# Holding input loads behind the crossbar transposes of the batch in work

## The chip, the cores and the metric

The kernel runs on one core of a Trainium2 chip. The metric is the device time in microseconds (us) of one execution. Times are medians of several executions, and comparisons use executions in the undisturbed ("fast") state, taken in the same rounds on the same chip. Batches are counted from 0, as in the code: the "batch four" that the prediction mentions is batch 3.

## The reference

Eight batches of attention (8 heads, 576 tokens, head size 64) with a relative bias, followed by a feed-forward layer that takes the largest of three products:

```python
scores = scale * np.matmul(q, k.transpose(0, 1, 3, 2)) + bias      # per batch and head
attn = np.exp(scores - scores.max(-1)); attn /= attn.sum(-1) + 1e-09
attn_out = np.matmul(attn, v)                                       # (8, 8, 576, 64)
x = attn_out.transpose(0, 2, 1, 3).reshape(8 * 576, 512)
h = np.maximum(np.maximum(x @ w1, x @ w2), x @ w3)                  # 512 -> 768
out = h @ w_out                                                     # 768 -> 512
```

## The kernel before

For each batch three kinds of transfer matter here. GpSimd issues the loads of q, k and v from HBM, with a cast from float32 to bfloat16. SyncE issues the crossbar transposes of the loaded q and k into `qT` and `kT`: DMA transfers that turn a tile on its way, four whole tiles and a tail (the last 64 tokens) for each. TensorE computes scores from `qT` and `kT` and products with v. Every load goes through `in_turn`, so GpSimd issues in program order.

```python
def load_qk(b, behind=None):          # 8 tile loads, then the tails of q and k: 11 loads
    ...
    go_behind(loads, behind)          # every load waits for the transfer `behind`

def load_v(b, h0, h1, behind=None):   # 4 tile loads and 2 tails: 6 loads
    ...

def transposes(b):                    # SyncE: tile t of q and of k, five steps
    for t in range(KT + 1):
        one(0, t)                     # records turned_qk[b, 0, t]
        one(1, t)                     # records turned_qk[b, 1, t]
        yield
```

In the main loop over batches b and head pairs hp, the transposes of batch b + 1 are issued step by step during batch b from hp 1 on, the fourth tile (`t = KT - 1`) in the second half of hp 2 and the tail in hp 3. The loads stand between them:

```python
if hp == (2, 1, 0)[min(b, 3) - 1] and b + 1 < B:
    load_v(b + 1, 0, H, turned_qk[2, 1, KT - 1] if b == 1 else None)
if (b, hp) == (2, 0):
    batch[3] = load_tiles()
    load_qk(3, divided[1, HP - 1, 1])
if hp == 2 and 1 < b < B - 2:
    batch[b + 2] = load_tiles()
    load_qk(b + 2)
```

So q and k of batch 4 and later wait for nothing but free buffers and their turn.

The softmax here doesn't subtract the row's maximum and nothing guards it: scores larger than these inputs give would overflow.

Of the kernel before, what the change touches and what calls it, by code (L numbers as in the profile page):

```python
# [39 lines left out]
def kernel(  # L40
# [13 lines left out]
    B, H, S, D = q.shape  # L54
# [8 lines left out]
    KT = 4  # L63
# [63 lines left out]
    def main_part(src, b):  # L127
        return src[b, :, 0 : KT * P, :].rearrange("h (t p) d -> p t h d", p=P)

    def tail_part(src, b, h0, h1, par):  # L130
        return src[b, h0 + par : h1 : 2, KT * P : S, :].rearrange("h p d -> p h d")

    def in_turn(b, load):
        return inorder(load)

    def load_main(src, b, h0, h1, dst, t0=0, t1=KT):
        x = main_part(src, b)
        return [
            in_turn(b, nc.gpsimd.dma_start(out=dst[:, t, h0:h1, :], in_=x[:, t, h0:h1, :])) for t in range(t0, t1)  # L139
        ]  # L140
# [5 lines left out]
    def load_q_tail(b):  # L146
        dst = qtail[b % 2][0 : S - KT * P].rearrange("p g (h d) -> p (g h) d", h=2)
        return in_turn(b, nc.gpsimd.dma_start(out=dst, in_=q[b, :, KT * P : S, :].rearrange("h p d -> p h d")))

    def k_diag(b, par, h0, h1):  # L150
        return diag(ktail[b % 2], par, h0, h1)
# [4 lines left out]
    def load_tail(src, b, h0, h1, dst):  # L156
        return [
            in_turn(b, nc.gpsimd.dma_start(out=dst(b, par, h0, h1), in_=tail_part(src, b, h0, h1, par)))
            for par in range(2)
        ]  # L160

    def load_qk(b, behind=None):

        loads = []
        for t in range(KT):
            for src, dst in zip((q, k), batch[b]):
                loads.append(in_turn(b, nc.gpsimd.dma_start(out=dst[:, t], in_=main_part(src, b)[:, t])))  # L167
        loads.append(load_q_tail(b))
        for par in range(2):
            load = nc.gpsimd.dma_start(out=k_diag(b, par, 0, H), in_=tail_part(k, b, 0, H, par))  # L170
            loads.append(in_turn(b, load))
        go_behind(loads, behind)

    def go_behind(loads, behind):

        for load in loads if behind else ():
            tc.add_manual_dep(
                load.ins, behind.ins.name,
                mybir.DependencyInfo(mybir.DependencyClass.Sync, mybir.DependencyReason.DATA),
                reason="these loads go behind the transposes in line",  # L180
            )

    def load_v(b, h0, h1, behind=None):
        loads = load_main(v, b, h0, h1, vx[b % 2][:, :, :, 0:D])
        go_behind(loads + load_tail(v, b, h0, h1, v_diag), behind)
# [224 lines left out]
    def store_outputs():  # L410

        while stores:
            stores.pop(0)()
# [7 lines left out]
    def early():  # L421

        if pending and None in pending[0][1]:
            n, fns = pending[0]
            i = fns.index(None)
            for fn in fns[:i]:
                fn()
            pending[0] = (n, fns[i + 1 :])
# [16 lines left out]
    def transposes(b):  # L445

        made = qk_tiles()
        qk.append(made)

        def one(j, t):  # L450
            n = P if t < KT or j else S - KT * P
            src = batch[b][j][:, t].rearrange("p h d -> p (h d)") if t < KT else (
                (qtail, ktail)[j][b % 2][0:n].rearrange("p h c -> p (h c)")
            )
            turned_qk[b, j, t] = inorder(nc.sync.dma_start_transpose(out=made[j][:, :, P * t : P * t + n], in_=src))  # L455

        for t in range(KT + 1):
            one(0, t)
            one(1, t)
            yield  # L460
# [59 lines left out]
    def times_band(hp, e4, t, lo, hi, put=lambda x: x):  # L520
        lo, hi = max(lo, P * t - P), min(hi, P * t + 2 * P)
        if lo < hi:
            c0, c1 = BAND - (hi - P * t + P), BAND - (lo - P * t + P)
            put(nc.vector.tensor_tensor(  # L524
                out=e4[:, t, :, lo:hi], in0=e4[:, t, :, lo:hi],
                in1=hank[:, 2 * hp : 2 * hp + 2, c0:c1][:, :, ::-1], op=ALU.mult,
            ))
# [17 lines left out]
    def visit(qT, kT, e4, c, mid=None, el=None):  # L545

        if el is not None:
            banks = [ps_a.tile([P, KT * 64], F32, tag="a", name="scq") for _ in range(2)]
            turn_left_queries(qT, kT, banks)
            put_left_queries(el, banks)  # L550
        for tt in range(0, KT, 2):
            sc = ps_s.tile([P, 2, 2, QS], F32, tag="sc", name="sc")
            for t in range(2):
                for par in range(2):
                    r = slice(64 * par, 64 * par + 64)
                    mm(
                        sc[:, par, t, :], lhsT=kT[r, P * (tt + t) : P * (tt + t) + P],
                        rhs=qT[r, c * QS : c * QS + QS],
                    )
            exp(e4[:, tt : tt + 2, :, c * QS : c * QS + QS].rearrange("p t h q -> p h t q"), sc[:])  # L560
            if tt == 0 and mid:
                mid()
# [30 lines left out]
    divided, turned_qk = {}, {}  # L593
# [62 lines left out]
    def x_tile():  # L656
        return xs.tile([P, KT + 1, d_model], BF16, tag="x_sb", name="x_sb")
# [3 lines left out]
    def next_late():  # L661
        return late.pop(0)() if late else (lambda: None)

    def e_tiles():
        return (
            ep.tile([P, KT, 2, QM], BF16, tag="e4", name="e4"),
            ep.tile([P, S + KT * P], BF16, tag="el", name="el"),
        )
# [75 lines left out]
    for hp in range(HP):  # L744
# [14 lines left out]
        def keys():  # L759
            left_keys(hp, qT, kT, el, QS, S)  # L760
# [33 lines left out]
    for b, hp in [(b, hp) for b in range(1, B) for hp in range(HP)]:  # L794
        if hp == 0:
            x_sb[b] = x_tile()
        qT, kT = (x[:, hp, :] for x in qk[b])
        e4, el = e_tiles()
        together = b > 1 and (b, hp) != (2, 0)
        rate = 8 if b == 1 or (b, hp) == (2, 0) else 13  # L800



        visit(qT, kT, e4, 0)
        store_outputs()
        if b == 1:
            if hp == 0:
                crossbar = transposes(2)
            next(crossbar, None)
        elif hp and b + 1 < B:  # L810
            if hp == 1:
                crossbar = transposes(b + 1)
            next(crossbar)
        early()
        if turned:
            turned.pop(0)()
        quotients = next_late()
        times_band(hp, e4, 0, 0, QS, inorder)
        quotients()
        if b == 1 and hp + 1 < HP:  # L820
            spread_packed(hp + 1, nc.vector)

        def keys():
            left_keys(hp, qT, kT, el, 0, S)
            if together:
                next_late()()

        fill(rate, keys, *([lambda: None] if together else []))
        times_bandt(hp, el)


        visit(qT, kT, e4, 1, el=el if together else None)
        store_outputs()
        if b == 1 or hp in (1, 2) and b + 1 < B:
            next(crossbar, None)
        early()
        if turned:
            turned.pop(0)()
        if not together:
            quotients = next_late()  # L840
            times_band(hp, e4, 1, 0, QM, inorder)
            quotients()
        if b == 1 and hp + 1 < HP:
            second_transposes(qk[1], hp + 1)
        if hp == 1:
            add_ffn((b - 1) * CH if b > 1 else QS, CH if b > 1 else QS)
        if hp == (2, 1, 0)[min(b, 3) - 1] and b + 1 < B:
            load_v(b + 1, 0, H, turned_qk[2, 1, KT - 1] if b == 1 else None)
        if (b, hp) == (2, 0):
            batch[3] = load_tiles()  # L850
            load_qk(3, divided[1, HP - 1, 1])
        if hp == 2 and 1 < b < B - 2:
            batch[b + 2] = load_tiles()
            load_qk(b + 2)

        def queries():
            if not together:
                left_queries(hp, qT, kT, el)
            times_band(hp, e4, 3, 0, QM, inorder)

        def bands_2():
            for t in range(1 if together else 2, 3):
                times_band(hp, e4, t, 0, QM, inorder)

        fill(rate, bands_2, queries)
        times_band_left(hp, el)
        for half in range(2):
            late.append(lambda b=b, hp=hp, e4=e4, el=el, half=half: attend(b, hp, e4, el, half))
# [44 lines left out]
```

## Time and profile before

| | before |
|---|---|
| median time | 325.49 us (325.08 to 326.58, 3 runs) |
| span of the profiled execution | 324.7 us |
| TensorE busy | 305.5 us (94%) |
| share of 16 DMA engines' span taken by GpSimd's queue | 78.1% |
| landing of a k transpose, median | 8.2 us |
| TensorE's named waits for `kT` | 1.87 + 0.22 us at batch 3, 1.09 us at batch 4 |

How to read it: TensorE carries the time, so an idle stretch of it is worth its length, and idle time of the others is worth nothing. The share of the DMA queue sums the time that the packets took, and it can pass 100%, so it shows crowding and not how much the engines could still move.

### The profile page before, as it was taken

The numbers are of one execution on the slowest core, as the hardware profiler recorded it, in microseconds if no ns is written. First come the engines' busy times: TensorE is split into PE (matmuls) and PEld (weight loads), VectorE is DVE, ScalarE is ACT, GpSimd is POOL, SyncE is SP. The second block draws the span as 40 slices with busy tenths as digits, with TensorE's granted clock in tenths as the row PEclk, the third lists the DMA queues.
The fourth block names the chain that finished last, engine by engine and source line by source line (L and its number), as shares of the span: only waits on it lengthen the run. The fifth ranks groups of instructions, "written<-read, shape, count | busy, mean of one in ns | idle before, by whom it ended". The sixth has DMA issues, their size and how long they took to land.

```text
span 324.7 us, 8194 instructions
## 1 busy us (share of the span) xinstructions
PE 305.5 (94%) x3288; PEld 171.1 (53%) x3328; DVE 214.1 (66%) x535; ACT 201.1 (62%) x297; POOL 108.1 (33%) x143
## 2 busy tenths in 40 slices
PE   7768999999979999899999999999999999999995
PEld 2346777765535555455555555555555554444442
DVE  6476788776665676676777766776667675454452
ACT  4958898886766667576777677767776661121221
POOL 8941980459557561285019500500000000000000
PEclk9979999999999999999999999999999999999999
DMA  9999999999999999999969998997031103301103
GB/s 164 200 206 198 149 134 176 113 119 158 194 164 156 126 197 168 109 117 176 195 73 135 150 192 88 123 202 99 12 75 71 62 2 73 131 0 65 67 0 129
DMA packets 163878, 40.34 MB, mean 124 GB/s; under 512 B 153720, under 2 KB 159360, under 8 KB 163840
## 3 DMA queue, kind: packets, MB, share of 16 engines
q0 software_dynamic: 103776, 16.66, 78.1%
q1 hardware_dynamic: 58304, 22.69, 39.3%
q10 hardware_dynamic: 1760, 0.47, 0.7%
q8 instruction: 26, 0.43, 0.6%
q14 instruction: 12, 0.10, 0.1%
HBM read 35.39 MB, written 9.45 MB: 138 GB/s over the span
## 4 chain that ended last, share of the span: by engine, by line
PE 74%; DMA 8%; SPq 5%; ACT 4%; POOL 3%; DVE 3%; issue 2%; ACTq 0%; POOLq 0%
PE ps L94 38%; PE a L94 12%; PE pso L94 12%; PE sc L94 7%; DMA kT<-ktail 5%; SPq L455 4%; ACT e L530 3%; PE sct L94 2%; DMA vt<-in_v_dram 2%; PE scq L94 2%; DVE e L524 1%; POOL q_sb L139 1%; POOL vx L139 1%; DMA out_dram<-osb 1%; PE tp L97 1%
## 5 line engine op out<-in xcount | busy, mean ns | idle before, releaser
L94 PE MATMUL ps<-xT,w_bf 128*128 128x512 bf16 (+1 forms) x694 | 151.2, 357 | 1.4
L530 ACT ACTIVATE e<-sc 128x1024 bf16<-128x1024 f32 x128 | 124.5, 1033 | 20.5 <-PE sc L94 20.5
L94 PEld LDWEIGHTS <-w_bf 128*128 128x128 bf16 x720 | 65.2, 97 | 64.1 <-issue 8.4
L524 DVE TENSOR_TENSOR e<-e,hank 128x512 bf16<-128x512 bf16 (+2 forms) x136 | 59.0, 470 | 14.3 <-ACT e L530 12.9
L339 ACT ACTIVATE m<-ps 128x512 bf16<-128x512 f32 x54 | 32.9, 609 | 52.3 <-PE ps L94 52.3
L345 DVE TENSOR_TENSOR m<-ps,m 128x512 bf16<-128x512 f32 x54 | 37.1, 687 | 34.0 <-PE ps L94 34.0
L94 PEld LDWEIGHTS <-kT 64*128 64x128 bf16 (+1 forms) x832 | 29.7, 95 | 40.0 <-issue 23.2
L94 PE MATMUL pso<-wo_bf,hT 128*128 128x512 bf16 (+2 forms) x208 | 47.7, 373 | 0.8 <-issue 0.2
L350 DVE TENSOR_TENSOR hT<-ps,m 128x512 bf16<-128x512 f32 x54 | 37.2, 688 | 16.5 <-PE ps L94 15.1
L139 POOL DMA_DIRECT2D vx<-in_v_dram x32 | 28.3, 902 | 59.1 <-PE a L94 44.5
L94 PE MATMUL a<-vx,e 128*128 128x65 bf16 x1024 | 46.0, 195 | 0.0
L94 PE MATMUL sc<-qT,kT 64*128 64x256 bf16 x512 | 40.8, 272 | 4.9 <-DMA kT<-k_sb 1.9
L94 PEld LDWEIGHTS <-e 128*128 128x128 bf16 x1024 | 41.7, 99 | 0.9
L94 PE MATMUL a<-vt,el 128*128 128x130 bf16 x160 | 35.9, 224 | 2.4 <-DMA vt<-in_v_dram 2.4
L110 DVE COPY osb<-pso 128x512 f32<-128x512 f32 (+1 forms) x33 | 22.6, 686 | 18.0 <-PE pso L94 14.3
L530 ACT ACTIVATE el<-scq 128x256 bf16<-128x256 f32 (+1 forms) x55 | 20.5, 416 | 21.3 <-PE scq L94 21.3
L632 DVE TENSOR_TENSOR x_sb<-a,rd 128x256 bf16<-128x256 f32 (+1 forms) x64 | 31.4, 491 | 2.2
L94 PEld LDWEIGHTS <-hT 128*128 128x128 bf16 x222 | 20.1, 98 | 22.4 <-issue 1.5
L94 PEld LDWEIGHTS <-el 128*128 128x128 bf16 x416 | 24.2, 97 | 11.6 <-issue 5.3
L530 ACT ACTIVATE el<-sct 128x576 bf16<-128x576 f32 (+2 forms) x36 | 21.6, 603 | 10.3 <-PE sct L94 9.1
L167 POOL DMA_DIRECT2D q_sb<-in_q_dram x24 | 21.9, 913 | 10.5 <-DMA vx<-in_v_dram 4.0
L167 POOL DMA_DIRECT2D k_sb<-in_k_dram x24 | 21.9, 912 | 9.1 <-DMA vx<-in_v_dram 8.8
(68 smaller groups left out, 156.8 us busy)
## 6 DMA issues: line engine op xcount, KB each, us to landing
out_dram<-osb SPq DMA_DIRECT2D x35, 256.0 KB, 3.0
vx<-in_v_dram POOLq DMA_DIRECT2D x32, 128.0 KB, 6.5
q_sb<-in_q_dram POOLq DMA_DIRECT2D x26, 128.0 KB, 8.4
k_sb<-in_k_dram POOLq DMA_DIRECT2D x24, 128.0 KB, 9.1
w_bf<-in_moe_w_dram POOLq DMA_DIRECT2D x3, 768.0 KB, 13.5
xT<-in_k_dram SPq DMA_DIRECT2D x6, 128.0 KB, 4.9
hank<-w_dr SPq DMA_DIRECT2D x2, 384.0 KB, 6.1
wo_bf<-in_moe_w_out_dram POOLq DMA_DIRECT2D x1, 768.0 KB, 11.9
```

What stands on the lines that cost most here:

```text
L94: inorder(nc.tensor.matmul(*args, **kw))
L97: inorder(nc.tensor.transpose(*args))
L110: return inorder(nc.vector.tensor_copy(out_, in_))
L139: in_turn(b, nc.gpsimd.dma_start(out=dst[:, t, h0:h1, :], in_=x[:, t, h0:h1, :])) for t in range(t0, t1)
L167: loads.append(in_turn(b, nc.gpsimd.dma_start(out=dst[:, t], in_=main_part(src, b)[:, t])))
L339: nc.scalar.activation(out=st[fb]["m0"][:], in_=ps0, func=ACTF.Copy)
L345: inorder(nc.vector.tensor_tensor(out=m[:], in0=ps1, in1=st[fb]["m0"][:], op=ALU.max))
L350: inorder(nc.vector.tensor_tensor(out=hT[:, fb * CH : fb * CH + CH], in0=ps2, in1=st[fb]["m"][:], op=ALU.max))
L455: turned_qk[b, j, t] = inorder(nc.sync.dma_start_transpose(out=made[j][:, :, P * t : P * t + n], in_=src))
L524: put(nc.vector.tensor_tensor(out=e4[:, t, :, lo:hi], in0=e4[:, t, :, lo:hi], in1=hank[:, 2 * hp : 2 * hp + 2, c0:c1][:, :, ::-1], op=ALU. ...
L530: nc.scalar.activation(out=out_, in_=in_, func=ACTF.Exp, scale=inv_sqrt_d)
L632: divided[b, hp, half] = inorder(nc.vector.tensor_tensor(out=x_sb[b][:, 2 * half : 2 * half + n, P * hp : P * hp + P].rearrange("p t (h d) ...
```

## The change

The intent is to keep loads that nobody needs yet from running beside the transposes that TensorE needs next. v of batch 3 moves from hp 1 to hp 2 of batch 2 and waits for the fourth k transpose of batch 3. The q and k of batches 4 to 7 wait for the fourth k transpose of the batch before them.

```diff
-        if hp == (2, 1, 0)[min(b, 3) - 1] and b + 1 < B:
-            load_v(b + 1, 0, H, turned_qk[2, 1, KT - 1] if b == 1 else None)
+        if hp == (2, 2, 0)[min(b, 3) - 1] and b + 1 < B:
+            load_v(b + 1, 0, H, turned_qk[b + 1, 1, KT - 1] if b < 3 else None)
         ...
         if hp == 2 and 1 < b < B - 2:
             batch[b + 2] = load_tiles()
-            load_qk(b + 2)
+            load_qk(b + 2, turned_qk[b + 1, 1, KT - 1])
```

## The prediction

> **What bounds the kernel now.** Batches are numbered from 0 as in the code, so "batch four" of the title is batch 3. I read the page's first two parts, then busy time by stage, then TensorE's own waits, then the chain that ended last around those waits, and last the DMA queues. TensorE is busy 305.5 us of a span of 324.7 at a granted clock of 0.995, so only its idle time can be won. Busy time by stage (columns: window, its length, then busy time of TensorE, weight load, VectorE, ScalarE, GpSimd, clock, DMA share, GB/s):
>
> ```profile
> 75.00:92.00 17.00, 16.32 (x200) 9.11 (x202) 11.48 (x28) 11.91 (x18) 11.30 (x15) 1.00 1.91 180
> 92.00:109.00 17.00, 14.80 (x170) 7.92 (x168) 10.89 (x26) 11.68 (x17) 11.90 (x16) 1.00 2.13 152
> ...
> 126.00:143.00 17.00, 15.81 (x163) 8.01 (x165) 10.90 (x26) 11.68 (x17) 7.87 (x10) 1.00 1.62 128
> 143.00:160.00 17.00, 16.84 (x200) 9.32 (x200) 12.16 (x31) 11.42 (x17) 6.45 (x9) 1.00 1.92 169
> 160.00:177.00 17.00, 16.84 (x198) 9.23 (x198) 11.82 (x29) 12.51 (x19) 7.69 (x10) 1.00 1.21 109
> ```
>
> A settled window has 16.84 of 17, that is 0.16 idle. Two windows have more: 92 to 109 has 2.20 and 126 to 143 has 1.19. From 143 to 262 every such window is settled, so loads there hide nothing that can be won. The first 40 us (8.9 us idle) come before anything the change touches. TensorE's instructions in order show what the two bad windows wait for:
>
> ```profile
> 94.94 0.50 PE L94 MATMUL sc<-qT,kT 64*128 64x256 bf16 x6
> 97.31 0.28 PE L94 MATMUL sc<-qT,kT 64*128 64x256 bf16 x2 [1.87 <-DMA kT<-k_sb]
> ...
> 99.38 0.42 PE L94 MATMUL sct<-qT,kT 128*128 128x512 bf16 x2 [0.22 <-DMA kT<-ktail]
> ```
> ```profile
> 134.22 0.42 PE L94 MATMUL sct<-qT,kT 128*128 128x512 bf16 x2 [1.09 <-DMA kT<-ktail]
> ```
>
> These are the first scores of batch 3 and of batch 4: the fourth tile and the tail of k have not come through the crossbar. Together 1.87 + 0.22 + 1.09 = 3.18 us. The chain at the first of them (start, length, what) shows why:
>
> ```profile
> 86.41 1.21 SPq L455
> 87.72 2.12 SPq L455
> 89.93 1.21 SPq L455
> 91.24 8.10 DMA kT<-ktail
> ```
>
> SyncE issues the transposes back to back here (each starts 0.1 us after the one before ended), and the last takes 8.1 us to land. One issue takes 2.12 and another, at 83.24, 2.45, against the usual 1.2. What that latency is when no loads run, the DMA answers for two stretches say: 107 to 128, beside the q and k loads of batch 5, and 212 to 226, when all loads are over.
>
> ```profile
> kT<-k_sb SPq DMA_TRANSPOSE x4, 8.5
> ```
> ```profile
> kT<-k_sb SPq DMA_TRANSPOSE x3, 2.4
> ```
>
> So the latency is mostly queueing beside the loads. GpSimd's instructions say which loads stand in the way (start, time, load):
>
> ```profile
> 78.49 1.89 POOL L139 DMA_DIRECT2D vx<-in_v_dram  x2
> ...
> 86.29 0.89 POOL L167 DMA_DIRECT2D q_sb<-in_q_dram  x1 [1.92 <-DMA ktail<-in_k_dram]
> ...
> 107.88 0.90 POOL L167 DMA_DIRECT2D q_sb<-in_q_dram  x1
> ```
>
> The values of batch 3 go out from 78.49 to 84.4 and q and k of batch 4 from 86.29 to 101.4, across the transposes of batch 3 (74.56 to 99.3). The q and k of batch 5 go from 107.88 to 126.7, across the transposes of batch 4 (105.68 to 134.2).
>
> **What the Trainium skill says.** "DMA: Bandwidth & Descriptors", section "Issuing engines are not separate DMA queues": transfers from any engine run on the same 16 DMA engines and interleave. The trace agrees: 8.5 us beside GpSimd's loads, 2.4 without, for transposes that SyncE issues. Section "Queues, rings and completion order" of that page says that each DMA engine takes turns between the queues that have work, a packet at a time; so putting a transpose first in line takes keeping the load from being issued, as this change does. Section "Anatomy of one DMA — SWDGE (gpsimd) path" says that the wait for a semaphore is on the issuing sequencer. So a new wait holds all later loads of GpSimd too; the trace shows that order, as q of batch 5 (107.88) starts only when the v of batch 4, itself held until 101.88, is out. "Perfetto Trace Analysis", section "DMA Instruction — HWDGE (DVE, Sync)", says that the movement lies outside the recorded instruction: here 1.2 us of issue against 8.1 to landing.
>
> **The change part by part.** I compared the instruction order of both kernels: it is the same on all five engines, apart from names. Only waits are added, at one load of v and at the first q and k loads of three blocks. No transfer, byte or computation is added or removed.
>
> Part one: v of batch 3 waits for the fourth k transpose of batch 3; q and k of batch 4, behind it in GpSimd's order, are held by the same wait. With 78 to 90 free of new loads, the transposes at 83.24 and 87.72 should take the usual 1.2 to issue. SyncE was back to back, so this moves the later ones up: 2.45 − 1.2 = 1.25, so the fourth k is issued at about 86.5, and the tail 1.25 + 0.92 = 2.17 earlier, at 89.1. With 2.4 to 4 us to land, the fourth k is there at 89 to 90.5 (wanted at 95.44) and the tail at 91.5 to 93 or, if v is beginning beside it, 96 (wanted at 99.16 − 1.87 = 97.3). Both waits go: −2.09 us.
>
> What it costs: v of batch 3 begins at about 89.5 in place of 78.5. Its six loads take 4 × 0.87 + 2 × 0.65 = 4.8 us to issue, to 94.3, and 6.5 to 7.6 us to land (medians of the page, vx and vt), so all is in by about 102. It is first read by the product at 107.2, now 105.1: 3 us of slack. The 11 loads of q and k of batch 4 follow, 94.3 to about 104. Their first tile lands at about 103; its transpose was issued at 105.68, now 103.6. The fourth tile goes out around 101 to 103, lands by 112, and its transpose comes at about 118.
>
> Part two: q and k of batch 5 wait for the fourth k transpose of batch 4, issued at 122.51 before. Between the end of v of batch 4 (about 110 issued, 118 landed) and about 121 the transposes have the engines to themselves, so the tail, which landed at 134.17, should land near 126 to 127, where 131 is needed: −1.09 us. The loads of q and k of batch 5 then go out at about 122 to 133, ahead of v of batch 5, which TensorE holds until 135.7 anyway. First use by a transpose was at 140.37: 7 us and more later than the first landing.
>
> Part three: q and k of batches 6 and 7 move up or down by a few us: before, they go out at 140.4 and 174.0, behind v; now at the landing of the fourth k transpose, which was issued at 155.3 and 189.3, so at about 155 and 189. Their 11 loads end by about 165 and 199, and v of the next batch, held until 169.3 and 203.3 by TensorE, isn't delayed. No TensorE wait lies there now: 0 us.
>
> Sum: −2.09 − 1.09 = −3.18 us, all on the path, because TensorE carries it and everything after it is settled. 325.49 − 3.18 = 322.3.
>
> **The rivals.** First: v of batch 3 becomes the new wait. It was 11 us too early and is now 3 us early by my estimate; if the fourth k transpose lands at 95 instead of 90, TensorE waits 2 to 3 us at the first product of batch 3 and the time stays at 324.5 to 325.5. For it: v took 12.3 us (median of 78 to 85) when it met transposes. Against: then it stood beside both the q and k loads still landing and the transposes. Second: the crowd only moves: v of batch 4 and the held q and k of batch 4 now run together from 94 to 118, beside the first transposes of batch 4, and the tail of k still comes late; then only part one's 2.1 us are won: 323.4. Against: 15 us lie between the last such load and the need. Third: the transposes are slow from the q and k loads of their own batch, which the change does not move; then little changes, 325. Against: at 91.24, 13 us after the last of those loads was issued (77.3 to 78.6), the tail still took 8.1 us.
>
> **Range and chances.** The most that can be won is the 3.18 us of named waits, 1.0%, so over 2% faster is almost out of reach. The three runs of before spread over 1.5 us. The likely failures give back 1 to 3 us. I take 322.4, with 321.4 to 324.6 for 8 in 10; faster by 2% 0.01, within 2% 0.97, slower by 2% 0.02 (only if the late v stalls several batches).
>
> **What would show it.** In the changed kernel's stages 92 to 109 and 126 to 143, TensorE's idle time falls from 2.20 and 1.19 to about 0.2 each, with no wait for the DMA into kT. The k transposes of batch 3 land in under 5 us instead of 8. GpSimd shows a wait of about 10 us for the transpose before v of batch 3, and its loads of q and k for batches 5 to 7 start near 122, 155 and 189. I am wrong if TensorE waits for vx or vt at about 105, if SyncE's issues stay at 2.1 to 2.5 us, or if a wait for kT stays at 131.

## The result, and the profile after

The changed kernel took 323.06 us (322.73 to 323.62, 4 runs) against 325.75 us (325.08 to 326.58, 4 runs) in the same comparison. The ratio is 0.9918, with a 95% interval of 0.9889 to 0.9947, so the change is faster beyond the noise, by 0.5 to 1.1%. Ratios are the mean time of one kernel's fast runs over that of the other's in the same rounds, so not quite the ratio of the medians. The predicted time was 322.4 us, with a range of 321.4 to 324.6.

Busy time by stage of the changed kernel, in the two windows that were bad before (columns: window, its length, busy time of TensorE, weight load, VectorE, ScalarE, GpSimd, clock, DMA share, GB/s):

```profile
92.00:109.00 17.00, 16.84 (x194) 9.08 (x192) 12.31 (x30) 12.35 (x20) 14.87 (x19) 1.00 1.92 127
126.00:143.00 17.00, 16.84 (x189) 9.13 (x191) 11.88 (x29) 12.34 (x19) 12.47 (x15) 1.00 1.74 116
```

Both now have the 16.84 us of a settled window, where before they had 14.80 and 15.81. That is 2.04 + 1.03 = 3.07 us more work done in the same time. TensorE's instructions at the first scores of batch 3 in the changed kernel carry no wait any more:

```profile
94.93 0.61 PE L94 MATMUL sc<-qT,kT 64*128 64x256 bf16 x8
...
96.95 0.41 PE L94 MATMUL sct<-qT,kT 128*128 128x512 bf16 x2
```

The eight matmuls that came as six and two with 1.87 us between are now one group. SyncE's issues ahead of them in the changed kernel (start, length, what):

```profile
83.06 2.55 SPq L455 DMA_TRANSPOSE kT<-k_sb  x1
85.70 0.54 SPq L381 DMA_DIRECT2D out_dram<-osb  x1
86.33 1.21 SPq L455 DMA_TRANSPOSE qT<-q_sb  x1
87.63 1.22 SPq L455 DMA_TRANSPOSE kT<-k_sb  x1
88.94 1.20 SPq L455 DMA_TRANSPOSE qT<-qtail  x1
90.24 2.24 SPq L455 DMA_TRANSPOSE kT<-ktail  x1
```

They start within 1 us of where they were; the gain is in what follows an issue. The DMA answer for 86 to 101 of the changed kernel (what, issuer, how many, us to landing) has the fourth k transpose and the tail at 2.8 and 4.5 us. The answer for the same stretch of the kernel before has them at 9.6 and 8.1:

```profile
kT<-k_sb SPq DMA_TRANSPOSE x1, 9.6
...
kT<-ktail SPq DMA_TRANSPOSE x1, 8.1
```

The changed kernel:

```profile
vx<-in_v_dram POOLq DMA_DIRECT2D x4, 128.0 KB, 4.2
...
vt<-in_v_dram POOLq DMA_DIRECT2D x2, 32.0 KB, 3.5
...
kT<-k_sb SPq DMA_TRANSPOSE x1, 2.8
...
kT<-ktail SPq DMA_TRANSPOSE x1, 4.5
```

The held v lands fast as well, in 4.2 us (tiles) and 3.5 us (tails) by medians; in the kernel before, the medians of the same loads were 12.3 and 13.5 us. GpSimd's instructions show the holds (start, time, load, idle time before it and what ended it):

```profile
91.00 3.53 POOL L139 DMA_DIRECT2D vx<-in_v_dram  x4 [12.41 <-PE ps L94]
...
127.64 0.89 POOL L167 DMA_DIRECT2D q_sb<-in_q_dram  x1 [13.20 <-DMA kT<-ktail]
...
188.13 0.90 POOL L167 DMA_DIRECT2D q_sb<-in_q_dram  x1 [14.82 <-DMA kT<-k_sb]
```

The releaser in the first two lines is a guess of the profile (the waiting load depends on the fourth k transpose, and something else happened to end nearby), so read the start and the idle time there, not the name.

The two profiled spans differ by 324.7 − 321.0 = 3.7 us, more than the two windows give: 0.43 us of the rest lie in the first 40 us (31.14 against 31.57 us busy), before anything the change touches.

### The profile page after: what moved, and what is told of

It reads as the page before. It is cut to its first block, busy times and chain, and to the rows that moved or that the text cites. A ratio compares the mean times of both kernels' runs of the same rounds, so it can differ in the third digit from the quotient of the medians.

```text
span 321.0 us, 8195 instructions
## 1 busy us (share of the span) xinstructions
PE 305.3 (95%) x3288; PEld 170.7 (53%) x3328; DVE 213.6 (67%) x535; ACT 201.1 (63%) x297; POOL 108.0 (34%) x143
## 2 busy tenths in 40 slices
DMA packets 163878, 40.34 MB, mean 126 GB/s; under 512 B 153720, under 2 KB 159360, under 8 KB 163840
## 3 DMA queue, kind: packets, MB, share of 16 engines
HBM read 35.39 MB, written 9.45 MB: 140 GB/s over the span
## 4 chain that ended last, share of the span: by engine, by line
PE 83%; DMA 7%; ACT 4%; POOL 3%; issue 1%; POOLq 0%; ACTq 0%
PE ps L94 44%; PE pso L94 13%; PE a L94 13%; PE sc L94 8%; DMA xT<-in_q_dram 5%; ACT e L530 3%; PE sct L94 2%; PE scq L94 2%; DMA vx<-in_v_dram 2%; POOL q_sb L139 1%; PE tp L97 1%; DMA out_dram<-osb 1%; ACT el L530 1%; POOL ktail L158 0%; POOL w_bf L683 0%
## 5 line engine op out<-in xcount | busy, mean ns | idle before, releaser
L94 PE MATMUL a<-vx,e 128*128 128x65 bf16 x1024 | 45.0, 193 | 0.0
L94 PEld LDWEIGHTS <-e 128*128 128x128 bf16 x1024 | 40.7, 97 | 0.9
```

What stands on the lines that cost most here:

```text
L94: inorder(nc.tensor.matmul(*args, **kw))
```

## The experiments

All kernels gave the right result but one. Since the executions of the kernel before spread over several us on some chips, the verdicts rest on TensorE's waits for `kT` in each profile, with the times beside them. Each of these is one execution; how far a wait differs from one execution to the next is shown under "The kernel before, three more profiles".

### The change again

> The changed kernel itself, for a tighter number. Theory (the three named waits of TensorE for kT, 1.87 + 0.22 + 1.09 = 3.18 us, are removed and nothing takes their place): 3.0 to 3.4 us faster than before, ratio 0.990. Rival (something gives back half a microsecond, as 323.06 against 325.75 hinted): 2.5 to 2.8 us faster, ratio 0.992.

It took 322.68 us (6 runs), ratio 0.990 (0.9837 to 0.9962), one run slow. The profile has no wait for `kT` and a span of 321.0 us again. The ratio lies at what the theory gave, but the interval (1.2 to 5.3 us of 326.5) holds the rival's half microsecond too; that difference stays below what the runs resolve.

### Only v of batch 3 held

```diff
# against the kernel before: the first part of the change alone
+        if hp == (2, 2, 0)[min(b, 3) - 1] and b + 1 < B:
+            load_v(b + 1, 0, H, turned_qk[b + 1, 1, KT - 1] if b < 3 else None)
```

> Only the new wait of v of batch 3 is made; q and k of batch 4 are held with it by GpSimd's order, q and k of batch 5 are not held. Theory (a transpose is late when loads are in flight beside it): batch 3's waits go, 2.09 us; the q and k of batch 5 now follow v of batch 4 directly, from about 115 us on, over the fourth k and tail transposes of batch 4, so the wait of 1.09 us stays or grows to 1 to 3 us: in all 0.5 to 2.1 us faster. Rival (delaying v of batch 3 alone brings everything): 3.2 us faster.

324.29 us, ratio 0.9924 (0.9878 to 0.9969). Batch 3 has no wait, batch 4 still has one, of the size that the theory allowed (TensorE's instructions of this run):

```profile
131.85 0.42 PE L94 MATMUL sct<-qT,kT 128*128 128x512 bf16 x2 [1.07 <-DMA kT<-ktail]
```

So this part is worth the 2 us of batch 3: 2.2 us by medians, with an interval of 1.0 to 4.0. In this kernel q and k of batch 5 went out from 111.9 to 129, across the tail of batch 4, which took 8.5 us to land.

### Only q and k held

```diff
# against the kernel before: the second part of the change alone
+            load_qk(b + 2, turned_qk[b + 1, 1, KT - 1])
```

> Only q and k of batches 4 to 7 wait for the preceding batch's fourth k transpose; v of batch 3 goes out at 78.5 as before. Theory (what matters is what is in flight from about 86 us on, when the fourth k and the tail of batch 3 are transposed; v of batch 3 has landed by about 91): both waits go, 2.9 to 3.2 us faster, no different from the whole change. Rival (v of batch 3 is the load that crowds the transposes): part of the 2.09 us stays, 1.1 to 2.5 us faster, with a wait for kT at 95 to 99 us.

326.71 us, ratio 0.9991 (0.9944 to 1.0038), which excludes the 0.990 that my theory gave. The rival was right about the cause: the wait of batch 3 is all but unchanged, and only that of batch 4 is gone. The 1.1 to 2.5 us that it promised do not show: the interval runs from 1.8 us faster to 1.2 us slower.

```profile
97.36 0.28 PE L94 MATMUL sc<-qT,kT 64*128 64x256 bf16 x2 [2.00 <-DMA kT<-k_sb]
```

The DMA answer for 78 to 92 of this run says why. From 86.6 us on, when the last tail of k of batch 3 has landed, nothing but v of batch 3 is left of GpSimd's loads until 97.87, and yet:

```profile
vx<-in_v_dram POOLq DMA_DIRECT2D x4, 128.0 KB, 12.8
vt<-in_v_dram POOLq DMA_DIRECT2D x2, 32.0 KB, 13.8
...
kT<-k_sb SPq DMA_TRANSPOSE x3, 8.9
```

The six loads of v, issued from 78.4 to 84.7, take 12.8 us (tiles) and 13.8 us (tails) by medians to land beside the transposes, the last at about 97.7 (84.10 + 13.56). They stand beside the transposes until the fourth k has landed (97.3), where I had assumed that they had landed by 91. The fourth k transpose took 9.3 us here and 9.6 in the kernel before, where q and k of batch 4 were queued behind v. More loads waiting in the same queue hardly made it slower; that some load of that queue was in flight did. The opposite case, v out of the way and only q and k of batch 4 beside these transposes, was not run.

### Only q and k of batch 5 held

```diff
+            load_qk(b + 2, turned_qk[b + 1, 1, KT - 1] if b == 3 else None)
```

> Only q and k of batch 5 wait, for the fourth k transpose of batch 4. Theory: the wait of 1.09 us at the first tail score of batch 4 goes and the 2.09 us of batch 3 stay: 1.0 to 1.1 us faster. Rival (the two are linked: the late start of batch 3 hid part of batch 4's wait, or the other way round): 0 or 2 us.

326.39 us, ratio 0.9986 (0.994 to 1.0031). In the profile the wait of batch 4 is gone and those of batch 3 are there (1.63 + 0.30 us). The time, with an interval of 3 us, cannot tell 1 us from 0. Nor does the missing wait say much by itself: it is missing too in two profiles of kernels without this hold (the next run, and the fourth profile of the kernel before). What separates the two is the landing of batch 4's k tail: 3.4 us here and 2.4 us in the run before this one, against 7.1 to 8.6 us in all six profiles without the hold.

### Only q and k of batches 6 and 7 held

```diff
+            load_qk(b + 2, turned_qk[b + 1, 1, KT - 1] if b > 3 else None)
```

> Only q and k of batches 6 and 7 wait. Theory (no wait of TensorE lies in their transposes before the change): 0, within 0.3 us of before; the transposes of batches 5 and 6 land some us sooner all the same. Rival (shorter queues help the rest too): 0.5 us or more faster.

325.99 us, ratio 0.9966 (0.9925 to 1.0008): no difference that the runs resolve, though the medians differ by 0.8 us, on the rival's side. The fourth k transposes of batches 5 and 6 landed in 2.3 us instead of about 10, as expected. But the profile brought a surprise: batch 3 waited 1.80 + 0.16 us, and batch 4 not at all, although this kernel runs as the one before up to 155 us.

### v of batch 3 behind q and k of batch 4

```diff
# against the changed kernel, at batch 2
-            load_v(3, 0, H, turned_qk[3, 1, KT - 1])   # then q and k of batch 4
             load_qk(4, turned_qk[3, 1, KT - 1])
+            load_v(3, 0, H)
```

> The changed kernel with the order turned at one place: q and k of batch 4 first, v of batch 3 behind them. It measures how late v of batch 3 may come. Theory (v has about 3 us of slack by my estimate, its first reader is at 105.1 us): v goes out 9.5 us later, from about 100.5 to 105.5, and lands at about 112, so TensorE waits 6 to 8 us for vx or vt at 105: slower than the changed kernel by 6 to 8 us, than before by 3 to 5. Rival (v's slack is much larger than I reckoned): under 2 us slower than the changed kernel.

332.63 us, ratio 1.0177 (1.0127 to 1.0227): 5.9 us slower than the kernel before by medians, a little over the 3 to 5 expected. TensorE's instructions show a wait within the 6 to 8 us of the theory, and its cause:

```profile
111.42 0.29 PE L94 MATMUL a<-vt,el 128*128 128x130 bf16 x1 [6.77 <-DMA vt<-in_v_dram]
```

The wait is not the whole loss: the profiled span is 9.1 us longer than that of the changed kernel. TensorE also ran slowly after the wait. The granted clock was 0.50 from 111 to 114 us and 0.57 from 114 to 117, and 1.00 again after that; from the first tail score at 112.51 to the next at 122.79 it took 10.28 us, against 8.33 in the changed kernel:

```profile
109.00:126.00 17.00, 14.58 (x162) 8.63 (x164) 7.36 (x19) 6.33 (x9) 1.25 (x2) 0.80 1.22 131
```

After the shorter waits of the kernel before (1.87 us, in the window 92 to 109) the clock shown is 1.00. So here the long wait cost some 2 us more than its length; why the clock fell was not tested.

So the order behind the hold matters: v of batch 3 is needed at about 105 us and must be the first load let go. In this kernel its tails were issued at 102.6 to 104 and landed in about 8 us. With v first, as in the change, the tails are issued by 95.8 and the last lands at about 98.4, with 6.4 us to spare before the first reader at 104.76.

### The later v held too

```diff
-        if hp == (2, 2, 0)[min(b, 3) - 1] and b + 1 < B:
-            load_v(b + 1, 0, H, turned_qk[b + 1, 1, KT - 1] if b < 3 else None)
+        if hp == 2 and b + 1 < B:
+            load_v(b + 1, 0, H, turned_qk[b + 1, 1, KT - 1])
```

> The changed kernel with v of batches 4 to 7 held as well, each until the fourth k transpose of its batch. It asks whether the time left has anything to do with the loads. Theory (all kT waits are gone, the DMA no longer sets any of TensorE's time after 40 us): the same as the changed kernel within 0.3 us, with the fourth k and tail of batch 4 landing in under 5 us instead of some 7. Rival (what v of batch 4 does beside the transposes still costs, or the held loads now come too late for q and k of the next batch): 0.5 us or more in either direction.

323.0 us, ratio 0.9878 (0.9841 to 0.9916), run on another chip than the first four. No wait for `kT`, and the tail of batch 4 landed in 3.5 us instead of the 5.5 us of the changed kernel, but the time is that of the changed kernel on the other chips (322.68 and 323.06): these transposes were in time already. The profiled execution was the slowest of the six (325.41 us) and has a wait of 1.65 us for v of batch 2 at 73 us, a load that every version here holds behind the fourth k transpose of batch 2. There v was let go at 63.97, 0.55 us after the fourth k transpose had landed (63.42), and its tail landed at 73.14. So a hold can cost, too, in some executions.

### No v from batch 3 on, a wrong result

```diff
+            if b == 1:
                 load_v(b + 1, 0, H, turned_qk[2, 1, KT - 1])   # no other load of v
```

> The changed kernel without any load of v from batch 3 on, so with 30 fewer loads (4.7 MB less read) and a wrong result on purpose: batches 3 to 7 use the v of batches 1 and 2. It puts a floor under what fewer or better placed loads could win. Theory: the same as the changed kernel within 0.3 us. Rival (DMA queueing still costs somewhere): 0.5 us or more faster.

322.5 us, ratio 0.9865 (0.9819 to 0.991), with the result wrong. The 30 loads are 5.9 MB by the profiles' pages (29.49 MB read against 35.39), not the 4.7 that the expectation says. Against 323.0 us of the kernel above on the same chip, leaving them out brings 0.5 us by medians, less than these few runs resolve. It says nothing of the q and k loads, which stayed; but the changed kernel's two profiles show no TensorE wait for any DMA after the first 40 us.

### The kernel before, three more profiles

> The kernel before, unchanged, for a second profile. The wait for the tail of k of batch 4 (1.09 us in the first profile) was not there in the profile of the kernel that holds only the late loads, although nothing differs until 155 us. Theory A (that wait is marginal: the tail lands within about 1 us of when it is wanted, so it is there in some executions only, while the roughly 2 us of batch 3 are in all): waits for kT of 1.9 to 2.2 us at batch 3, and of 0 to 1.3 us at batch 4. Theory B (both are fixed): 2.1 and 1.1 us.

> The kernel before once more. Theory A: about 2 us at batch 3 again, another value between 0 and 1.3 us at batch 4. Theory B: 2.1 and 1.1 us.

> The kernel before a third time. Theory A: about 2 us at batch 3, 0 to 1.3 us at batch 4. Theory B: 2.1 and 1.1 us.

These are single executions, whose state is unknown by the rule for one core. TensorE's waits for `kT` in all four profiles of the kernel before, read from its instructions in order, and the spans:

| profile of before | batch 3, us | batch 4, us | sum | span |
|---|---|---|---|---|
| first | 1.87 + 0.22 | 1.09 | 3.18 | 324.7 |
| second | 2.38 + 0.19 | 0.92 | 3.49 | 325.1 |
| third | 2.36 + 0.58 | 0.55 | 3.49 | 325.1 |
| fourth | 1.66 + 0.21 | 0 | 1.87 | 323.0 |

Theory A holds for batch 4 (0 to 1.09 us), and its band for batch 3 was too narrow: 1.87 to 2.94 us. On average 3.0 us are waited, 2.37 at batch 3 and 0.64 at batch 4. Span less waits is 321.5, 321.6, 321.6 and 321.1 us, all close to the 321.0 of both profiles of the changed kernel: the waits account for all but 0.1 to 0.6 us of the difference, in each execution by its own amount. The tails of batch 4 landed 7.1 to 8.6 us after their issue, within about 1 us of when TensorE wanted them. In the fourth profile, the tail was issued at 124.85 and took 7.1 us, to 131.95, and the score began at 132.52.

### v of batch 3 and q and k of batch 5 alone

```diff
# against the kernel before: the first part of the change, and
+            load_qk(b + 2, turned_qk[b + 1, 1, KT - 1] if b == 3 else None)
```

> Only two of the new waits: v of batch 3 (which holds q and k of batch 4 behind it), and q and k of batch 5. Theory (these two are the whole effect; q and k of batches 6 and 7 need no wait): no wait for kT at batches 3 and 4, the same time as the changed kernel, 322.5 to 323.3 us. Rival (the late waits matter too): a wait for kT at batch 5 or 6, 0.5 us or more slower than that.

323.81 us (4 runs), ratio 0.9929 (0.9841 to 1.0017). No wait at batches 3 and 4, but the rival's wait at batch 5 is there:

```profile
164.82 0.42 PE L94 MATMUL sct<-qT,kT 128*128 128x512 bf16 x2 [0.79 <-DMA kT<-ktail]
```

Its tail took 8.5 us to land, with q and k of batch 6 not held. In the four profiles of the kernel before, the tail of batch 5 landed 0.6 to 2.1 us ahead of its score. TensorE asked for it at 164.03 here, with the earlier waits gone, against 166.1 to 168.3 there. So without the late holds a wait can come up that the kernel before did not have. How often it comes, one profile of this kernel cannot say; the time lies 0.5 us above the upper end of the theory's range, and the changed kernel did not run in these rounds.

## Why the prediction was right, point by point

**The bound and the amount.** Right. The three named waits were TensorE's only waits for a transfer after the first 40 us, and all are gone in both profiles of the changed kernel. Over all profiles, the wait of batch 3 is there in the seven that do not hold v of batch 3 (1.9 to 2.9 us) and in none of the seven that do or leave it out; the wait of batch 4 is in four of the six that do not hold q and k of batch 5, and in none of the eight that do. The measured gain was 2.7 us by medians in the first comparison and 3.8 in the second, about the 3.18 us predicted. That number is one execution's: the waits are 1.87 to 3.49 us from execution to execution, 3.0 on average, and that the first profile lay near the mean was luck. The steps below were off by 1 to 6 us in several places without changing the sum, because a landing that is early by much wins no more than one that is early by little.

**Part one, −2.09 us.** The sum was right, and the run with v of batch 3 alone held shows that this hold carries it. In the working, "the transposes at 83.24 and 87.72 should take the usual 1.2 to issue" failed for the first (2.55 us at 83.06) and held for the second (1.22 against 2.12). That "SyncE's issues stay at 2.1 to 2.5 us" was one of the prediction's own signs of being wrong; it came true in part (2.24 us for the tail, too) and did no harm. So the fourth k was issued at 87.63 and not 86.5, and the tail at 90.24 and not 89.1: the 2.17 us of earlier issue came out as 0.1 us for the fourth k and 1.0 for the tail, and the gain came mostly from the landing. The fourth k landed in 2.8 us, at 90.4, just inside the 89 to 90.5 given, and the tail at 94.8, between the two cases given for it. "The k transposes of batch 3 land in under 5 us" held for these two only; the first three took 5.8 to 7.9.

**What part one costs.** "3 us of slack" for v was too little by half, the trace has 6.4: I had used the page's medians of 6.5 to 7.6 us to landing, which include crowded loads, where the held v took 3.5 to 4.2. (That v "was 11 us too early" was a misreading: its last load landed at 97.6, 9.6 us ahead of its reader at 107.2.) The first rival, v as the new wait, did not come; the run with v second shows its size, 6.77 us.

**Which loads crowd.** The prediction named v of batch 3 and q and k of batch 4 together and did not choose. Before the third experiment I chose wrongly, and the run showed v to be enough. The statement of the Trainium skill ("DMA: Bandwidth & Descriptors", section "Queues, rings and completion order") that each engine takes turns between the queues that have work fits this. The latency followed whether the other queue had work: for the fourth k of batch 3 it was 9.3 us with v only, 9.6 with more behind it, and 2.3 to 3.9 in the seven profiles in which v is held or left out. That taking turns is the mechanism was not tested by itself.

**Part two, −1.09 us.** Right in outcome, mis-sized in time. "The tail … should land near 126 to 127" was 123.45 + 5.54 = 128.99, and q and k of batch 5 went out at 127.64 and not about 122, which was the time of the transpose's issue and not of its landing. The term that failed is "v of batch 4 (about 110 issued, 118 landed)": it was issued from 105.9 to 114.4 and took 12.3 us beside the transposes, to about 126. So the second rival, the moved crowd, was half true: the fourth tiles of batch 4 still had company, and the tail came 1.5 us before its score at 130.52, not 4 to 5. Its reserve was enough.

**Part three, 0 us.** No effect that the runs resolve, as said, but partly by luck: "No TensorE wait lies there now" did not reckon with TensorE asking 2 to 4 us earlier once the other waits are gone. Without these holds one profile has a wait of 0.79 us there.

**The third rival**, that a batch's own q and k loads are what slows its transposes, fits the earlier tiles only: the four k transposes of batch 3 still had a median of 6.3 us after the change, the fourth of them 2.8.

## What to carry to other kernels

A transfer on the path can be made late by others that nobody needs yet. Here they sat in different queues, and it was enough that the other queue had some work at that moment; how much more waited behind hardly mattered. Find the first instruction that needs the urgent transfer, hold the others until it has landed, and let go first whatever is needed first. Read such waits from several profiles: a wait that hangs on a landing within 1 us of its need comes and goes, and its mean is not what one profile shows.

## What the Trainium skill lacked or had wrong

- "DMA: Bandwidth & Descriptors", section "DMA Transpose (X-bar)", gives no time to landing: a transpose of four 128x128 tiles took 2.3 to 3.9 us to land with no load of GpSimd in flight (the fourth k of batch 3 in the kernels that hold v or leave it out) and 9.3 to 10.2 us beside loads of another queue (the same one in the four profiles of the kernel before: 9.6, 10.2, 9.3 and 9.5).
- The same page, section "Anatomy of one DMA — SWDGE (gpsimd) path", fits 2.0 us + bytes / 436e3. For the 128 KB of one v tile that is an estimate of 2.3 us. The first of the held v tiles of batch 3 took 3.6 us beside two tail transposes, the four 4.2 us by median, and in the kernel before, beside more transposes, they took 12.3 us. The fit is for one DMA and has no term for others in flight; these loads also move rows of 64 values and cast them, and which of the two makes the 3.6 us was not tested.
- The same page, section "Issuing engines are not separate DMA queues", says that transfers interleave, but not that their order alone can be worth 0.8% of a kernel bound by TensorE: both kernels moved 40.34 MB in 163878 packets.
- No page says when an issue of a k transpose on SyncE takes 2.5 us instead of 1.2. It took 2.54 us at 215.1 in the changed kernel too, when all q and k loads were over, so those loads cannot be its only cause; the cause stays open.
